# Four output quarters around the start of tile 1, the out-projection weights one place earlier, and a batch's score steps one block sooner, in a fused local-attention + SwiGLU kernel

## The chip, the cores and the metric

The kernel runs on one core of a Trainium2 chip. The metric is device time in microseconds (us), the median of five runs. Beside those five runs stands one profiled execution, whose trace gives every instruction's start and duration, and every DMA's issue and landing.

## What is computed

Two blocks follow each other. First comes attention with a sliding window of 96 keys and 8 global keys, with a bias that falls linearly with distance, over 4 batches, 8 heads, 768 positions and 64 features a head. Its output, read as 3072 tokens of 512 features, goes through a SwiGLU feed-forward block.

```python
keep = is_global | is_local                       # 8 first keys, or 0 <= rel < 96
scores = scale * q @ k.T - slopes * dist          # per head, masked where not keep
a = softmax(scores)
x = (a @ v).transpose(0, 2, 1, 3).reshape(3072, 512)
g = x @ w_gate                                    # 512 x 1536
out = (g * sigmoid(g) * (x @ w_val)) @ w_out      # 1536 x 512
```

## The kernel before, in words

**Tiles.** The 3072 tokens are cut in 8 tiles of 384 (t = 0 to 7), two tiles a batch. The 1536 hidden features are cut in 12 blocks of 128 (f = 0 to 11). I write (t, f) for block f of tile t. For each block `gate_or_val` runs four gate products and four value products (L547) into two PSUM banks. ScalarE then takes tanh of the gate (`th`, L558), VectorE makes `sl` from both (L560), and VectorE multiplies `sl` with the value product into `hT` (L564). Twelve `hT` blocks of a tile make three output groups of 128 tokens; each group is cut in four quarters of three matmuls (`out_part`, L576, into bank `o0`). A quarter reads three blocks of `hT` and one of four loads of `wo` (`load_wo(0)` to `load_wo(3)`, L218). After the fourth quarter ScalarE copies the bank out (`osb`, L582), and SyncE (SP) starts the write (L583). There are 96 quarters; `outs` lists those of tiles 0 to 6 in order, and the list `stretches` (L769 to L775) says after which block how many are taken. Before the change the first comes after (1,4), and one follows each block from (1,5) on, five of them at (1,11). The last three groups, those of tile 7, follow at the end.

**Attention steps between the blocks.** The attention of the next batch is cut into steps that TensorE runs between two blocks, at keys such as (t, 4), after that block's quarters, or (t, 11, 1), ahead of its quarter number 1. `tr` transposes q and k of two heads (L273; copies out on ScalarE L281, on VectorE L285 and L288). `sc` makes the scores of up to three units (L379); the exponentials (L387, ScalarE) of the first unit come at once, those of the others and all mask multiplications (L395, L398) are put on the list `later`. `va` makes denominators and numerators (L439), evicts the numerators (L470), and puts `invert` (L449, L450), `spread` (L455) and two scalings (L475, which write the next tile's `xT`) on `later`. `run_later` takes one entry off ahead of each gate, each value and each quarter; `take`, which starts a step, first empties the list. `first(1, 1)` places batch 1's steps in tile 1; batches 2 and 3 have theirs in `both`, at (t,0), (t,5), (t,8), (t+1,0), (t+1,4), (t+1,8) for t = 2 and 4.

**PSUM.** Gate and value products rotate over three banks (`spare`), over seven from (0,9) to (1,2) (`widen`, `narrow`). The first of three score units takes two of the same banks. So TensorE can start a value product only when the `sl` of the block before has been made, and scores only when the last gate's `sl` has.

**Loads.** GpSimd (POOL) issues the loads with a cast, in program order, on one queue: q and k of batch 0, v, weights, `wo` 0 and 1, then q and k heads 0 to 3 of batch 1, the global rows (L181), `wo` 2 and 3, q and k heads 4 to 7, v of batch 1. SP and ScalarE issue the first q and k heads, the identity, the distances and the first global v rows (L110 to L115). [...]

**Block 0's second half.** In tile 0 the steps `trh` and `sch` transpose and score the second half of batch 0; `trh(2, 3, True)` at (0,3) puts both qT copies (L330) on ScalarE, and `sch` puts the second half's exponentials (L361) on `later`.

Of the kernel before, what the change touches and what calls it, by code (L numbers as in the profile page):

```python
# [16 lines left out]
WIN = 216  # L17
# [20 lines left out]
def kernel(  # L38
# [12 lines left out]
    nc = tc.nc  # L51
# [18 lines left out]
    const_dr = nc.inline_tensor(  # L70
        np.concatenate([np.eye(128, dtype=np.float16), dist_np], axis=1), name="consts")
# [26 lines left out]
    dist = sb.tile([128, 3 * WIN], FP16, name="dist")  # L98
    J2 = TB // 128
    q32 = sb2.tile([128, 2, J2 * D], FP32, name="q32", tag="qst")  # L100
# [4 lines left out]
    def half_of(src, half, h0, h1):  # L105
        return src[0, h0:h1, TB * half:TB * half + TB, :].rearrange(
            "h (p j) d -> p h (j d)", p=128)
# [1 line left out]
    vG32 = sb.tile([NG, H, D], FP32, name="vG32")  # L109
    nc.sync.dma_start(out=k32, in_=half_of(k, 0, 0, 2))  # L110
    nc.scalar.dma_start(out=ident, in_=const_dr.ap()[:, 0:128])
    nc.scalar.dma_start(out=q32, in_=half_of(q, 0, 0, 2))
    nc.sync.dma_start(out=dist[:, 0:2 * WIN], in_=const_dr.ap()[:, 128:128 + 2 * WIN])
    nc.sync.dma_start(out=vG32, in_=v[0, :, 0:NG, :].rearrange("h p d -> p h d"))
    nc.sync.dma_start(out=dist[:, 2 * WIN:], in_=const_dr.ap()[:, 128 + 2 * WIN:])  # L115

# [30 lines left out]
    def stage(b):  # L147
        qst[b] = sb2.tile([128, H, J * D], FP16, name="qst", tag="qst")
        kst[b] = sb2.tile([128, H, J * D], FP16, name="kst", tag="kst")

    def load_qk(b, h0, h1):
        for st, src in ((kst[b], k), (qst[b], q)):
            nc.gpsimd.dma_start(
                out=st[:, h0:h1, :],
                in_=src[b, h0:h1].rearrange("h (p j) d -> p h (j d)", p=128))
# [23 lines left out]
    def load_globals():  # L179
        for dst, src in ((kG, k), (vG[:, 1:], v)):  # L180
            nc.gpsimd.dma_start(  # L181
                out=dst.rearrange("p b h d -> p (b h) d"),
                in_=src[1:, :, 0:NG, :].rearrange("b h p d -> p (b h) d"))

    def copy_globals(b):
        nc.sync.dma_start(
            out=vSs[b][0:NG],
            in_=vG[:, b, :, :].unsqueeze(1).broadcast_to([NG, NCH, H, D]))
# [28 lines left out]
    def load_wo(g):  # L217
        nc.gpsimd.dma_start(  # L218
            out=wo[:, 3 * g:3 * g + 3, :],
            in_=moe_w_out[384 * g:384 * g + 384].rearrange("(f p) d -> p f d", p=128))  # L220
# [18 lines left out]
    def banks(name, dt=FP32):  # L239
        return [bank(name, dt) for _ in range(2)]  # L240

    def spare(name, dt=FP32):
        tag = state["x"][gv.get("n", 0) % len(state["x"])]
        gv["n"] = gv.get("n", 0) + 1
        return single(name, tag, dt)

    def single(name, tag, dt=FP32):
        return ps.tile([128, 512 if dt == FP32 else 1024], dt, name=name, tag=tag)
# [6 lines left out]
    later = []  # L255

    def run_later(n):
        for _ in range(n):
            if later:
                later.pop(0)()  # L260
# [339 lines left out]
    pairs = {(b, hp): Pair(b, hp) for b in range(B) for hp in range(NP)}  # L600
    quads = {(b, g): Quad(b, g) for b in range(B) for g in range(2)}
    for c in range(3):
        load_v_rest(0, c)
    nc.gpsimd.dma_start(
        out=vCut[NG:NG + cut], in_=v[0, :, 3 * KC:TB, :].rearrange("h p d -> p h d"))
# [17 lines left out]
    def p_tr(hp, kt, qt, q_eng):  # L623
        tr = [single("trs", t, FP16)[:, 0:TB] for t in (qt, kt)]
        pairs[0, hp].turn_half(0, tr)
        pairs[0, hp].copy_half(0, tr, V, q_eng)

    V, A = nc.vector.tensor_copy, nc.scalar.copy
# [2 lines left out]
        make_slope(nc.scalar.mul, h)  # L631
    A(out=q16[:, 0, 0:2], in_=q32)
    V(out=k16[:, 0, 0:2], in_=k32)
    A(out=vG[:, 0], in_=vG32)
    copy_globals(0)
    nc.sync.dma_start(out=vCut[0:NG], in_=vG[:, 0])
    p_tr(0, "x0", "x1", A)
    for h in range(4, 8):
        make_slope(nc.vector.tensor_scalar_mul, h)
    load_w(0, 2)  # L640
# [6 lines left out]
    load_w(8, 12)  # L647
    load_wo(0)
    load_wo(1)
    stage(1)  # L650
    load_qk(1, 0, 4)
    load_globals()
    load_wo(2)
    load_wo(3)
    load_qk(1, 4, 8)
    for c in range(NCH):
# [29 lines left out]
    def sc(b, *units):  # L686
        def step():
            for i, (hp, bk, *other) in enumerate(units):
                pair = pairs[b + 1 if other else b, hp]
                on_vector = pair.b < 2 or bk < 2 or hp % 2 == 0  # L690
                exps, mask = pair.scores(
                    bk, nc.vector if on_vector else nc.gpsimd,
                    [spare("sc") for _ in range(2)] if len(units) == 3 and i == 0
                    else banks("sc"))
                if i == 0:
                    exps()
                else:
                    later.append(exps)
                later.append(mask)
        return step  # L700

    def va(b, g, half):
        return lambda: quads[b, g].values(half, bank, nc.vector)
# [4 lines left out]
    def tr(b, hp):  # L708
        return pairs[b, hp].transposes

    def trh(h0, h1, by_engine):
        def step():
            b0, b1 = single("trs", "o0", FP16), spare("trs", FP16)
            (a, b), (c, d) = [(t[:, 0:TB], t[:, TB:2 * TB]) for t in (b0, b1)]
            k_eng = V if by_engine else A
            pair_of = [(h0, (c, a)), (h1, (d, b))] if by_engine else [(h0, (b, a)), (h1, (d, c))]
            for hp, tr in pair_of:
                pairs[0, hp].turn_half(1, tr)
            for hp, tr in pair_of:
                pairs[0, hp].copy_half(1, tr, k_eng, A)  # L720
        return step

    def sch(hp):
        def step():
            p = pairs[0, hp]
            scs = [p.bias(1, 0), p.bias(1, 1)]
            for which in range(2):
                p.scores_half(1, which, scs[which], which == 1)
        return step

    def fetch(b, *hps):
# [7 lines left out]
    def first(t, b):  # L739
        return {(t, 2): [tr(b, 0), tr(b, 1)],  # L740
                (t, 4): [sc(b, (0, 0), (0, 1), (1, 0))],
                (t, 6): [tr(b, 2), tr(b, 3)],
                (t, 7): [sc(b, (1, 1), (2, 0), (2, 1))],
                (t, 9): [sc(b, (3, 0), (3, 1))],
                (t, 10): [va(b, 0, 0)],
                (t, 11, 1): [va(b, 1, 0)]}

    def both(t, b):

        n = b + 1  # L750
        return {(t, 0): [sc(b, (0, 2), (1, 2), (2, 2)), fetch(n, 0, 1)],
                (t, 5): [sc(b, (3, 2), (0, 0, n), (1, 0, n)), fetch(n, 2, 3)],
                (t, 8): [vas(b, 1)],
                (t + 1, 0): [sc(n, (0, 1), (1, 1), (2, 0))],
                (t + 1, 4): [sc(n, (2, 1), (3, 0), (3, 1))],
                (t + 1, 8): [vas(n, 0)]}

    def second(t, b):
        return {(t, 0): [sc(b, (0, 2), (1, 2))], (t, 3): [sc(b, (2, 2), (3, 2))],
                (t, 7): [vas(b, 1)]}  # L760

    half1 = {(0, 1): [trh(0, 1, False)], (0, 2): [sch(0)],
             (0, 3): [sch(1), trh(2, 3, True)], (0, 5): [sch(2)], (0, 6): [sch(3)],
             (0, 7): [va(0, 0, 1)], (0, 8): [va(0, 1, 1)]}

    def ff(t, f0, f1, n_out=(0,)):
        return [(t, f, n_out[(f - f0) % len(n_out)]) for f in range(f0, f1)]

    stretches = [  # L769
        (ff(0, 0, 12), half1),  # L770
        (ff(1, 0, 5, (0, 0, 0, 0, 1)) + ff(1, 5, 11, (1,)) + [(1, 11, 5)], first(1, 1)),
        (ff(2, 0, 12, (1,)) + ff(3, 0, 12, (1,)), both(2, 1)),
        (ff(4, 0, 12, (1,)) + ff(5, 0, 12, (1,)), both(4, 2)),
        (ff(6, 0, 12, (1,)), second(6, 3)),
        (ff(7, 0, 12, (1,)), {})]  # L775

    loads, after = {}, {}

# [105 lines left out]
```

The softmax here doesn't subtract the row's maximum and nothing guards it: scores larger than these inputs give would overflow.

## Time and profile before

| what | value |
|---|---|
| median of five runs (lowest to highest) | 244.96 us (243.76 to 245.14) |
| the profiled execution: its own time, and the span of its trace | 244.84 us, 243.1 us |
| granted TensorE clock | 1.00 |
| PE (TensorE) busy | 234.5 us, 96% of the span |
| VectorE (DVE), ScalarE (ACT), GpSimd busy | 165.9, 129.6, 96.7 us |
| gate and value products, L547 | 77.1 and 76.6 us |
| output quarters, L576 | 72.8 us |

The 1.7 us between the span and the execution's own time lie outside the first and last instruction. Busy times of PE overlap, since matmuls are pipelined; what a matmul costs is the distance from its start to the next one's: four products of 384 columns take 0.65 us, a quarter (three matmuls of 512 columns) 0.64 us. In a timeline row the first number is the start, the second the duration of the group of like instructions, and in brackets stands the engine's idle time ahead of it with what ended it.

### The profile page before, as it was taken

How to read it: one execution, taken by the hardware profiler on the slowest of the kernel's cores; microseconds unless marked ns; L12 is line 12 of the kernel's file. 1: busy time of each engine (PE TensorE's matmuls, PEld its weight loads, DVE VectorE, ACT ScalarE, POOL GpSimd, SP SyncE). 2: the span in 40 equal slices, each digit the busy share in tenths (PEclk: the TensorE clock that was granted, in tenths of full speed). 3: DMA queues.
4: the chain of work that ended last, by engine and by line, in shares of the span. 5: the costliest groups of instructions: out<-in, count | busy, mean ns of one | idle time of the engine just before them, and what ended most of it. 6: DMA issues, size and time to landing. Idle time of an engine off the chain costs nothing.

```text
span 243.1 us, 6052 instructions
## 1 busy us (share of the span) xinstructions
PE 234.5 (96%) x2428; PEld 135.5 (56%) x2428; DVE 165.9 (68%) x354; ACT 129.6 (53%) x295; POOL 96.7 (40%) x117
## 2 busy tenths in 40 slices
PE   8799899799999999999999999999999999999994
PEld 4456566455555556555565556555655565555543
DVE  5675749879796768776786658776785568555610
ACT  5548586786864565366346464367336634333221
POOL 8998674728980000996062252700032213000000
PEclk9999999999999999999999999999999999999999
DMA  7999999999999585799309877941101101110122
GB/s 145 167 181 198 180 206 198 203 156 127 147 122 148 122 133 97 49 158 143 57 5 148 143 140 87 71 65 44 46 0 46 43 6 39 45 43 1 44 89 86
DMA packets 84612, 25.10 MB, mean 103 GB/s; under 512 B 72816, under 2 KB 81640, under 8 KB 84584
## 3 DMA queue, kind: packets, MB, share of 16 engines
q0 software_dynamic: 65296, 14.05, 66.6%
q1 hardware_dynamic: 18728, 10.30, 17.3%
q8 instruction: 19, 0.31, 0.5%
q10 hardware_dynamic: 560, 0.36, 0.5%
q14 instruction: 9, 0.07, 0.1%
HBM read 28.67 MB, written 6.29 MB: 144 GB/s over the span
## 4 chain that ended last, share of the span: by engine, by line
PE 84%; DMA 6%; POOL 5%; DVE 2%; issue 1%; ACT 0%; DVEq 0%; POOLq 0%
PE gps L547 25%; PE vps L547 24%; PE ops L576 23%; DMA wv<-in_moe_w_val_dram 3%; PE sc L379 3%; PE num L439 3%; DMA vS<-in_v_dram 3%; PE den L439 2%; POOL q L119 1%; PE trs L273 1%; POOL wg L213 1%; PE ops L592 1%; POOL k L119 1%; POOL wv L213 1%; DVE xT L475 1%
## 5 line engine op out<-in xcount | busy, mean ns | idle before, releaser
L547 PE MATMUL gps<-xT,wg 128*128 128x384 f16 x376 | 77.1, 327 | 2.1 <-DVE hT L564 1.7
L560 DVE SCALAR_TENSOR_TENSOR sl<-th,gps 128x384 f32<-128x384 f32 x94 | 52.0, 553 | 39.5 <-ACT th L558 39.2
L547 PE MATMUL vps<-xT,wv 128*128 128x384 f16 x376 | 76.6, 326 | 0.5 <-DMA wv<-in_moe_w_val_dram 0.4
L558 ACT ACTIVATE th<-gps 128x384 f32<-128x384 f32 x94 | 46.9, 499 | 52.7 <-PE gps L547 51.4
L576 PE MATMUL ops<-wo,hT 128*128 128x512 f16 x276 | 72.8, 379 | 0.0
L564 DVE TENSOR_TENSOR hT<-vps,sl 128x384 f16<-128x384 f32 x94 | 52.1, 554 | 8.7 <-DVE sl L560 0.5
L547 PEld LDWEIGHTS <-wg 128*128 128x128 f16 x384 | 35.1, 98 | 33.1 <-issue 3.6
L547 PEld LDWEIGHTS <-wv 128*128 128x128 f16 x384 | 37.5, 98 | 26.6 <-issue 1.3
L576 PEld LDWEIGHTS <-hT 128*128 128x128 f16 x276 | 26.9, 98 | 23.8
L387 ACT ACTIVATE at<-sc 128x432 f16<-128x432 f32 x72 | 33.2, 538 | 11.5 <-PE sc L379 11.5
L516 POOL TENSOR_TENSOR xT<-ns,rb 128x384 f16<-128x384 f32 x10 | 9.8, 995 | 66.5 <-DVE rb L455 55.5
L171 POOL DMA_DIRECT2D vS<-in_v_dram x28 | 24.7, 893 | 5.8 <-DMA kst<-in_k_dram 4.1
L582 ACT ACTIVATE osb<-ops 128x512 f32<-128x512 f32 x23 | 13.7, 597 | 22.0 <-PE ops L576 22.0
L398 POOL TENSOR_TENSOR at<-at,masks 128x864 f16<-128x864 f16 x4 | 7.3, 1822 | 23.8 <-ACT at L387 19.1
L398 DVE TENSOR_TENSOR at<-at,masks 128x864 f16<-128x864 f16 x20 | 12.1, 605 | 5.7 <-ACT at L387 5.7
L194 POOL DMA_DIRECT2D kst<-in_k_dram x16 | 13.9, 885 | 2.3 <-PE vps L547 1.7
L361 ACT ACTIVATE at<-sc 128x432 f16<-128x432 f32 (+2 forms) x32 | 11.7, 446 | 5.3 <-PE sc L350 5.3
L194 POOL DMA_DIRECT2D qst<-in_q_dram x16 | 13.7, 878 | 0.0
L512 ACT COPY ns<-num 128x384 f32<-128x384 f32 x20 | 8.1, 492 | 7.9 <-PE num L439 7.9
L439 PE MATMUL num<-at,vS 128*32 128x216 f16 (+6 forms) x560 | 11.1, 226 | 0.0
L395 DVE TENSOR_TENSOR at<-at,masks 128x432 f16<-128x432 f16 x24 | 8.1, 378 | 4.3 <-ACT at L387 4.3
L449 DVE STREAM_TRANSPOSE dT<-den 128x384 f32<-128x384 f32 x16 | 9.3, 581 | 1.6 <-PE den L439 1.1
(74 smaller groups left out, 178.5 us busy)
## 6 DMA issues: line engine op xcount, KB each, us to landing
out_dram<-osb SPq DMA_DIRECT2D x23, 256.0 KB
vS<-in_v_dram POOLq DMA_DIRECT2D x24, 120.0 KB, 5.8
wo<-in_moe_w_out_dram POOLq DMA_DIRECT2D x4, 384.0 KB, 10.4
qst<-in_q_dram POOLq DMA_DIRECT2D x16, 96.0 KB, 4.2
kst<-in_k_dram POOLq DMA_DIRECT2D x16, 90.0 KB, 4.2
wg<-in_moe_w_gate_dram POOLq DMA_DIRECT2D x4, 256.0 KB, 7.7
wv<-in_moe_w_val_dram POOLq DMA_DIRECT2D x4, 256.0 KB, 7.8
kst<-in_k_dram POOLq DMA_DIRECT2D x2, 384.0 KB, 12.1
```

The costliest lines, as they stand in the source:

```text
L171: nc.gpsimd.dma_start(out=vSs[b][NG:NG + n, c, :, :], in_=v[b, :, KC * c:KC * c + n, :].rearrange("h p d -> p h d"))
L194: nc.gpsimd.dma_start(out=st[b][p0:p0 + n, h // 2, :, h % 2, :], in_=src[b, h, 0:n * J].rearrange("(t p) d -> p t d", p=n))
L361: nc.scalar.activation(out=at[:, hi, 0:col + n], in_=sc[hi][:, 0:col + n], func=AF.Exp, scale=scale)
L387: nc.scalar.activation(out=at[:, hi, :], in_=sc[hi][:, 0:BANK], func=AF.Exp, scale=scale)
L398: mul_eng.tensor_mul(at, at, m[:, :, o:o + BANK])
L439: nc.tensor.matmul(dst[r, o:o + n], lhsT=ones[:, 0:32] if side is None else vals[:, 4 * g + j, side::2], rhs=pairs[b, 2 * g + j // 2].at[c ...
L547: nc.tensor.matmul(gv[f, which][:, 0:TB], lhsT=w[:, c, 128 * f:128 * f + 128], rhs=x_of(t)[:, c, :], start=(c == 0), stop=(c == NC - 1))
L558: nc.scalar.activation(out=th, in_=dst[:, 0:TB], func=AF.Tanh, scale=0.5)
L560: nc.vector.scalar_tensor_tensor(out=sl, in0=th, scalar=1.0, in1=dst[:, 0:TB], op0=AluOp.add, op1=AluOp.mult)
L564: nc.vector.tensor_mul(hTs[t][:, f, :], dst[:, 0:TB], gv["sl"])
L576: nc.tensor.matmul(ops, lhsT=hTs[t][:, f, 128 * i:128 * i + 128], rhs=wo[:, f, :], start=(f == 0), stop=(f == NFF - 1))
L582: nc.scalar.mul(out=osb, in_=ops, mul=0.5)
```

## The change

1. **Head.** On SP's queue the distances change places with the first q heads, which ScalarE's queue issued: q now follows k on SP, and the distances follow the identity on ScalarE. The cast of the global v rows moves behind the first qT copy in ScalarE's order; SP's copies of those rows (L186, L636) follow it.
2. **Tile 0.** In the step at (0,3) the second qT copy moves from ScalarE to VectorE, and the exponentials of heads 2 and 3 are no longer put off.
3. **Quarters.** One quarter comes after each of (0,10), (0,11), (1,0), (1,2). Then one comes after each of (1,4) to (1,9), and two after (1,10) and (1,11). Tile 1 takes two more by its end than before, so that from tile 2 on every quarter in the list stands two places earlier and (7,10) and (7,11) have none.
4. **Loads.** `load_wo(2)` comes ahead of batch 1's q and k.
5. **Batch 1's steps.** All but the first two come one block sooner, and the last one empties `later` at once.

```diff
-    nc.scalar.dma_start(out=q32, in_=half_of(q, 0, 0, 2))
-    nc.sync.dma_start(out=dist[:, 0:2 * WIN], in_=const_dr.ap()[:, 128:128 + 2 * WIN])
+    nc.scalar.dma_start(out=dist[:, 0:2 * WIN], in_=const_dr.ap()[:, 128:128 + 2 * WIN])
+    nc.sync.dma_start(out=q32, in_=half_of(q, 0, 0, 2))
...
+    p_tr(0, "x0", "x1", A)
     A(out=vG[:, 0], in_=vG32)
     copy_globals(0)
     nc.sync.dma_start(out=vCut[0:NG], in_=vG[:, 0])
-    p_tr(0, "x0", "x1", A)
...
     load_wo(1)
+    load_wo(2)
     stage(1)
     load_qk(1, 0, 4)
     load_globals()
-    load_wo(2)
     load_wo(3)
...
-            k_eng = V if by_engine else A
+            k_eng, last = (V, V) if by_engine else (A, A)
...
-                pairs[0, hp].copy_half(1, tr, k_eng, A)
+                pairs[0, hp].copy_half(1, tr, k_eng, A if hp == h0 else last)
...
-                p.scores_half(1, which, scs[which], which == 1)
+                p.scores_half(1, which, scs[which], which == 1 and hp != 1)
...
                 (t, 4): [sc(b, (0, 0), (0, 1), (1, 0))],
-                (t, 6): [tr(b, 2), tr(b, 3)],
-                (t, 7): [sc(b, (1, 1), (2, 0), (2, 1))],
-                (t, 9): [sc(b, (3, 0), (3, 1))],
-                (t, 10): [va(b, 0, 0)],
-                (t, 11, 1): [va(b, 1, 0)]}
+                (t, 5): [tr(b, 2), tr(b, 3)],
+                (t, 6): [sc(b, (1, 1), (2, 0), (2, 1))],
+                (t, 8): [sc(b, (3, 0), (3, 1))],
+                (t, 9): [va(b, 0, 0)],
+                (t, 10, 1): [va(b, 1, 0), lambda: run_later(len(later))]}
...
-        (ff(0, 0, 12), half1),
-        (ff(1, 0, 5, (0, 0, 0, 0, 1)) + ff(1, 5, 11, (1,)) + [(1, 11, 5)], first(1, 1)),
+        (ff(0, 0, 10) + ff(0, 10, 12, (1,)), half1),
+        (ff(1, 0, 4, (1, 0)) + ff(1, 4, 10, (1,)) + ff(1, 10, 12, (2,)), first(1, 1)),
...
-        (ff(7, 0, 12, (1,)), {})]
+        (ff(7, 0, 10, (1,)) + ff(7, 10, 12), {})]
```

More of the change, by code (lines that the diff above doesn't have):

```diff
@@ L692, in step @@
                     bk, nc.vector if on_vector else nc.gpsimd,
-                    [spare("sc") for _ in range(2)] if len(units) == 3 and i == 0
+                    [spare("sc") for _ in range(2)] if i == 0 and len(units) == 3
                     else banks("sc"))
```

## The prediction

> **What bounds the kernel now.** I read the page's slices first, then busy time by stage, then what TensorE (PE) waits for, then the timelines around each PE wait.
>
> ```profile
> PE   8799899799999999999999999999999999999994
> PEclk9999999999999999999999999999999999999999
> ```
> ```profile
> 28.00:44.00 16.00, 16.00 (x225) 9.97 (x224) 12.06 (x25) 10.88 (x28) 9.08 (x13) 1.00 1.36 199
> 44.00:47.00 3.00, 1.25 (x8) 0.66 (x7) 2.69 (x6) 1.62 (x5) 3.00 (x4) 1.00 1.25 204
> ```
> ```profile
> PE gps L547 <- DVE hT L564: 1.7, 1, 1.7
> ```
> ```profile
> 43.49 0.81 PE L547 MATMUL vps<-xT,wv 128*128 128x384 f16 x4
> 46.05 0.81 PE L547 MATMUL gps<-xT,wg 128*128 128x384 f16 x4 [1.75 <-DVE hT L564]
> ...
> 50.22 0.81 PE L547 MATMUL gps<-xT,wg 128*128 128x384 f16 x4
> 51.05 0.81 PE L547 MATMUL vps<-xT,wv 128*128 128x384 f16 x4
> ```
>
> PE is full in nearly every slice at full clock (the stage rows give length, then busy time and count of PE, PEld, DVE, ACT, POOL, then clock, DMA share, GB/s). In 44 to 47 us PE works 1.25 of 3.00 us while VectorE works 2.69: VectorE, still behind from scaling x for tile 1, frees no PSUM bank. So only PE's idle time is to be won. I take it start to start: a product begins 0.16 us after the one before, so the value product of 43.49 gives PE free at 44.14, and the gate of 46.05 comes 1.91 us late. At 51.05 the value starts 0.18 late (0.83 after its gate, not 0.65). At tile 2's first gate, (2,0), the fourth matmul waits for the last xT piece, 74.47 to 75.03: 0.30 late. From there to the end I find no start-to-start gap but about 0.10 wherever PE changes between full and smaller matmul shapes, and the change leaves their number alone. **At most 1.91 + 0.18 + 0.30 = 2.39 us can be won.**
>
> Ahead of 28 us PE waits for weights: its gate of 25.61 stops for wg (0.41 late) and the value product stops for wv until 27.62 (0.61). That chain is one load after another on POOL's queue.
>
> **The change, part by part.**
>
> *Head: 0.* PE's slack ahead of the weights is 0.41 + 0.61 = 1.0 us. ScalarE's cast of q waited 0.68 us, to 4.67, for q; its issue moves from 1.16 on ScalarE's queue to about 1.26 on SP's, behind k. [...] The vG cast (0.61) moves from 5.09 to about 6.1, ahead of the exponentials of 6.92; the copies SP issued at 5.73 and 6.64 come 1 us later and are read at 13.44. At (0,3) a qT copy goes from ScalarE (0.48) to VectorE (0.55), and exponentials (0.97) move ahead of a tanh: PE is waiting for weights there. 0.
>
> *Quarters in the gap.* A quarter is 3 x 213 ns = 0.64 us. With VectorE's order unchanged, PE runs: gate and value of (0,10) to 40.24, quarter to 40.88, (0,11) to 42.18, quarter to 42.82, (1,0) to 44.12, quarter to 44.76, (1,1) to 46.06. The gate of (1,2) then asks for its bank at 46.06 and VectorE frees it at 46.00 as before: the gap of 1.91 is filled by three quarters (1.92). `wo` loads 0 and 1 were issued at 28.80 and 29.79 with landings 8.8 and 9.7 us later (37.6, 39.5): in time. Load 2 takes the place of k's, 1.9 us behind load 1 (the spacing of two 384 KB loads): 41.4, in time for 44.12.
>
> The fourth quarter, after (1,2), is ready at 47.36 and needs load 3:
>
> ```profile
> 36.00 0.78 POOL L218 DMA_DIRECT2D wo<-in_moe_w_out_dram  x1 [0.42 <-DMA wv<-in_moe_w_val_dram]
> ```
> ```profile
> DMA to landing us min/median/max: 8.8/10.4/11.7
> ```
>
> 36.00 + 11.7 = 47.7. The bytes ahead of it on the queue are the same, so PE waits to 47.77: **-0.41** (between 0 and 1.0, should the order change its landing by half a us). Behind it wait the transposes, which start at 48.51 instead of 47.44. k and q of heads 0 to 3 land 1.9 later than their 41.5 and 43.6: in time. The bank wait of 51.05 shrinks to 0.04. So four quarters (2.56) are done for a lag of 0.93 at the scores of (1,4) (53.37 instead of 52.44): 1.91 + 0.18 - 0.41 - 0.04 = **+1.64**.
>
> *Output write.* The first 256 KB write now leaves SP near 49.2, and the globals' copies, issued at 44.46 before, are queued behind it; they are read after 65. q of heads 4 to 7 was issued at 39.82 and landed 14.3 later, 54.1; it is now read at 56.4. [...]
>
> *Transposes one block sooner.* They stood after (1,6), when all exponentials and masks of (1,4) were through. After (1,5) two entries are still on the list, and `take` runs them first: one pair of exponentials ahead of the kT copies, one mask (0.52) ahead of qT.
>
> ```profile
> 57.54 0.55 DVE L564 TENSOR_TENSOR hT<-vps,sl 128x384 f16<-128x384 f32 x1
> 58.01 0.95 DVE L285 COPY qT<-trs 128x768 f16<-128x768 f16 x1
> 58.88 0.17 DVE L288 COPY kT<-kT 128x56 f16<-128x56 f16 x1
> 58.96 0.95 DVE L285 COPY qT<-trs 128x768 f16<-128x768 f16 x1
> 59.82 0.32 DVE L288 COPY kT<-kT 128x56 f16<-128x56 f16 x1
> 59.94 0.56 DVE L560 SCALAR_TENSOR_TENSOR sl<-th,gps 128x384 f32<-128x384 f32 x1
> ```
>
> Before, transposes began at 57.09, this `sl` ended at 60.50, and the scores that take its bank started at 60.61: no slack left. After, transposes begin at 53.37 + 2.71 = 56.08. ScalarE's two exponential pairs run 55.28 to 57.07, masks 56.55 to 57.67 on VectorE, qT from 57.67: 1.59 behind the transposes, not 0.92. `sl` then ends at 57.67 + 2.49 = 60.16, the scores are due at 59.60: **-0.57** (0 to 1.1; about half if the mask overlaps, double if ScalarE slips by a kT pair).
>
> *Last steps sooner.* The values now follow (1,9) and (1,10), and the list is emptied at once. Before, from the start of the first values (67.80), the last xT ended at +7.23 and (2,0)'s fourth gate matmul was due at about +6.97. After, VectorE's order to xT is nearly the same (two pieces of hT work exchanged), and (2,0) starts at +7.10, its fourth matmul at +7.58: **+0.30**. `sl` and `hT` of (1,11) are queued behind the xT work; the `sl` ends at +7.70, and (2,0)'s value wants that bank at +7.75. No slack, but no wait.
>
> *Two places ahead for the rest.* Fourth quarters fall on f = 1, 5, 9 instead of 3, 7, 11. At (2,0), (3,0), (3,4) and the same places of tiles 4 and 5 the ScalarE copy `osb` (0.60, some 0.49 of the queue) now lies between the exponentials just put out and the next tanh:
>
> ```profile
> 78.17 0.49 ACT L558 ACTIVATE th<-gps 128x384 f32<-128x384 f32 x1 [0.17 <-PE gps L547]
> 78.55 1.79 ACT L387 ACTIVATE at<-sc 128x432 f16<-128x432 f32 x4
> 80.19 0.53 ACT L558 ACTIVATE th<-gps 128x384 f32<-128x384 f32 x1
> ```
>
> That queue is full; the tanh of 80.19 slips by 0.49 and by 0.09 for the quarter's end. Its `sl` ended at 81.32 and the value that needs the bank began at 81.86: slack 0.49 beside 0.05 of signalling. Six times 0.58 - 0.49: **-0.5** (0 to 1.2). (7,10) and (7,11) without quarters: 0.05 at one bank. The tail's own quarters cover the last hT (0.65 + 3 x 0.64 against 1.95).
>
> Sum: 1.64 - 0.57 + 0.30 - 0.5 - 0.05 = **0.82 us won**. Against the profiled execution, 244.84 - 0.82 = 244.02; the median stands 0.12 above that execution, so 244.96 - 0.82 = **244.1 us**.
>
> **Rivals.**
>
> *All won.* The tile 1 stall and the `osb` stalls do not appear, as `sl` runs a little sooner than I queue it: 0.82 + 0.57 + 0.5 = 1.89, 243.1 us. For it: both are differences of a few tenths. Against it: no slack in the `sl` of 59.94.
>
> [...]
>
> *Slower: full queues.* Work put ahead of a tanh or an `sl` in an order that cannot be changed costs more than the overlap I allow: 1.1 at the tile 1 scores and 0.25 at each of six places is 2.6 instead of 1.07, so 0.7 lost: 245.7 us. It decides once these places cost over 1.9 together. For it: the queues are full just there. Against it: the row of 0.49 slack.
>
> **How the numbers follow.** A measurement of this kernel tells about 0.3% (0.73 us) from no change. Forecast 0.44 (243.6 to 244.7, about half of it past 244.2 towards faster); all won 0.20; moved 0.16; slower 0.20. Faster 0.44 x 0.5 + 0.20 = 0.42; slower 0.18; same 0.40. The range, 243.0 to 245.6, reaches into both outer cases.
>
> **What would show it.** The PE wait for hT near 46 is gone; a wait for wo of about 0.4 near 47.4; scores of block (1,6) late by 0.6; no wait at (2,0); value products one block after (2,0), (3,0), (3,4) late by under 0.1. I am wrong if the fourth quarter waits over 1 us, if transposes wait for q, or if the `osb` places cost over 0.2 each.

## The result, and the profile after

The changed kernel takes 244.0 us (median of 28 runs, 243.19 to 246.35) against 244.84 us (47 runs of the kernel before): ratio 0.9973, interval 0.9962 to 0.9985. By the ratio 0.66 us are won (0.37 to 0.93); the two medians lie 0.84 apart; 0.82 was forecast. The profiled execution took 243.99 us, its span 242.2.

PE's slices, and the stage row that answers to the gap's (length; busy time and count of PE, PEld, DVE, ACT, POOL; clock, DMA share, GB/s). The slices, 6.1 us each, read as before: they are too coarse for a gap of 1.9 us; the row shows it closed.

```profile
PE   8899799999999999999999999999999999999994
```
```profile
44.00:47.00 3.00, 3.00 (x19) 1.72 (x18) 2.63 (x6) 2.11 (x6) 1.35 (x2) 1.00 1.36 194
```

VectorE still works 2.63 of these 3.00 us: it was not relieved, PE was given something else to do. The timeline of PE around the old gap (start, duration of the group):

```profile
44.61 0.81 PE L576 MATMUL ops<-wo,hT 128*128 128x512 f16 x3
45.25 0.81 PE L547 MATMUL gps<-xT,wg 128*128 128x384 f16 x4
45.90 0.81 PE L547 MATMUL vps<-xT,wv 128*128 128x384 f16 x4
46.55 0.81 PE L547 MATMUL gps<-xT,wg 128*128 128x384 f16 x4
47.24 0.81 PE L547 MATMUL vps<-xT,wv 128*128 128x384 f16 x4
47.88 0.81 PE L576 MATMUL ops<-wo,hT 128*128 128x512 f16 x3
```

The starts are 0.64, 0.65, 0.65, 0.69, 0.64 apart: no gap above 0.04. The fourth quarter starts as soon as its value product is through; the wait for `wo` that I forecast is not there. What the waits of PE show instead is the head (first the lines of before, then those of the changed kernel: us in all, times, longest):

```profile
PE gps L547 <- DMA wg<-in_moe_w_gate_dram: 0.2, 1, 0.2
PE vps L547 <- DMA wv<-in_moe_w_val_dram: 0.4, 1, 0.4
```
```profile
PE gps L547 <- DMA wg<-in_moe_w_gate_dram: 0.7, 1, 0.7
PE vps L547 <- DMA wv<-in_moe_w_val_dram: 0.7, 1, 0.7
```

The value product that ends PE's wait for weights starts at 28.09, not at 27.62 as before. So I compare two numbers per trace: when that product starts (**weights**), and the span from there on (**rest**), which hardly depends on how early the weights came (214.09 and 214.07 with weights at 28.09 and 29.02). e1 to e4, e5 to e8, e9 to e11 and e12 ran on four chips, each beside its own runs of the kernel before (medians 244.84, 244.85, 244.71 and 245.24 us); from row to row compare the ratios, not the times. One of e11's six runs (246.16 us, clock 0.992) counts as slow and is not in its ratio.

| kernel | time, us | ratio (interval) | weights | rest |
|---|---|---|---|---|
| before | 244.84 | 1 | 27.62 | 215.44 |
| changed | 244.0 | 0.9973 (0.9962-0.9985) | 28.09 | 214.09 |
| e1, head as before | 243.83 | 0.9961 (0.9945-0.9976) | 29.02 | 214.07 |
| e2, before with the new head | 244.91 | 1.0009 (0.9994-1.0025) | 27.57 | 215.56 |
| e3, output copy put off | 250.5 | 1.0231 (1.0205-1.0258) | 27.75 | 221.09 |
| e4, e3 with wo sooner, old head | 250.28 | 1.0218 (1.0190-1.0246) | 27.06 | 220.98 |
| e5, gap filled, nothing else | 245.94 | 1.0038 (1.0020-1.0056) | 27.88 | 215.47 |
| e6, steps as before | 246.47 | 1.0057 (1.0033-1.0081) | 27.60 | 218.10 |
| e7, two orders at the transposes | 243.37 | 0.9937 (0.9915-0.9960) | 27.83 | 213.74 |
| e8, quarters back in phase | 243.99 | 0.9960 (0.9945-0.9976) | 27.38 | 214.20 |
| e9, steps sooner alone | 245.1 | 1.0024 (1.0005-1.0043) | 27.51 | 215.69 |
| e10, third wo load late | 245.15 | 1.0024 (1.0004-1.0044) | 27.56 | 215.76 |
| e11, e7 with wo sooner | 243.2 | 0.9930 (0.9904-0.9957) | 27.83 | 213.60 |
| e12, e11 with the old head | 242.82 | 0.9899 (0.9871-0.9927) | 27.62 | 213.60 |

In the profiled executions the rest fell by 215.44 - 214.09 = 1.35, and weights that came 0.47 later took part of it back.

### The profile page after: what moved, and what is told of

It reads as the page before. It is cut to its first block, busy times and chain, and to the rows that moved or that the text cites. A ratio compares the mean times of both kernels' runs of the same rounds, so it can differ in the third digit from the quotient of the medians.

```text
span 242.2 us, 6053 instructions
## 1 busy us (share of the span) xinstructions
PE 235.2 (97%) x2428; PEld 135.7 (56%) x2428; DVE 165.9 (69%) x355; ACT 129.2 (53%) x294; POOL 96.7 (40%) x117
## 4 chain that ended last, share of the span: by engine, by line
PE 87%; DMA 8%; POOL 2%; ACT 1%; issue 1%; POOLq 0%
PE gps L547 26%; PE vps L547 25%; PE ops L576 24%; DMA wv<-in_moe_w_val_dram 6%; PE sc L379 3%; PE num L439 3%; DMA vS<-in_v_dram 3%; PE den L439 2%; PE trs L273 1%; PE ops L592 1%; POOL vS L171 1%; POOL k L119 1%; POOL q L119 1%; PE sc L339 0%; ACT at L387 0%
## 5 line engine op out<-in xcount | busy, mean ns | idle before, releaser
L560 DVE SCALAR_TENSOR_TENSOR sl<-th,gps 128x384 f32<-128x384 f32 x94 | 51.9, 552 | 39.9 <-ACT th L558 39.1
L387 ACT ACTIVATE at<-sc 128x432 f16<-128x432 f32 x72 | 33.9, 533 | 10.8 <-PE sc L379 10.8
```

The costliest lines, as they stand in the source:

```text
L387: nc.scalar.activation(out=at[:, hi, :], in_=sc[hi][:, 0:BANK], func=AF.Exp, scale=scale)
L560: nc.vector.scalar_tensor_tensor(out=sl, in0=th, scalar=1.0, in1=dst[:, 0:TB], op0=AluOp.add, op1=AluOp.mult)
```

## The experiments

**e1 and e2: the head.** e1 puts the head back in the changed kernel; e2 is the kernel before with the new head alone.

```diff
-    nc.scalar.dma_start(out=dist[:, 0:2 * WIN], in_=const_dr.ap()[:, 128:128 + 2 * WIN])
-    nc.sync.dma_start(out=q32, in_=half_of(q, 0, 0, 2))
+    nc.scalar.dma_start(out=q32, in_=half_of(q, 0, 0, 2))
+    nc.sync.dma_start(out=dist[:, 0:2 * WIN], in_=const_dr.ap()[:, 128:128 + 2 * WIN])
...
+    A(out=vG[:, 0], in_=vG32)
+    copy_globals(0)
+    nc.sync.dma_start(out=vCut[0:NG], in_=vG[:, 0])
     p_tr(0, "x0", "x1", A)
-    A(out=vG[:, 0], in_=vG32)
-    copy_globals(0)
-    nc.sync.dma_start(out=vCut[0:NG], in_=vG[:, 0])
```

> The changed kernel with the head as before: first q heads on ScalarE's queue, distances on SP's, the vG cast ahead of the first qT copy. In the changed kernel's trace the last weights that TensorE waits for ahead of 28 us landed at 28.04 instead of 27.57, and the fourth quarter found its wo load already there. Theory: the head edit made the weights 0.47 later, and the wait for the fourth wo load, which I had put at 0.41, was hidden under it. Then with the head back the weights land near 27.6, the fourth quarter waits about 0.4 for wo, and the time stays within 0.15 of the changed kernel: 243.9 to 244.1. Rival 1: the head costs and nothing hides it: 0.4 to 0.5 faster, 243.5. Rival 2: the later weights are chance of one execution: weights land anywhere from 27.5 to 28.1, time 244.0, and the wait for wo is there only when they land early.

> The kernel before with only the head edited (queues exchanged, vG cast behind the first qT copy). Theory: the head edit itself delays the weights; wv lands near 28.0, everything behind it moves along, 0.3 to 0.5 slower than before: 245.2. Rival (chance): wv lands near 27.6 and the time is that of before within 0.15: 244.8.

My theory that the head edit made the weights late falls. With the old head the wait for the weights ended even later, at 29.02; with the new head on the old kernel at 27.57. PE's waits of e1:

```profile
PE gps L547 <- DMA wg<-in_moe_w_gate_dram: 1.4, 1, 1.4
PE vps L547 <- DMA wv<-in_moe_w_val_dram: 0.7, 1, 0.7
```

Over all traces the wait ends at 27.06 to 29.02 with the old head (before, e1, e4, e5, e12; mean 27.84) and at 27.38 to 28.09 with the new (nine traces; mean 27.68). The landing scatters by more than the edit moves it: the second rival was right, though the scatter is wider than its 27.5 to 28.1. The rests of pairs that differ in the head agree (214.09 and 214.07; 215.44 and 215.56).

**e3 and e4: the output copy behind the tanh.** The six late value products are there in the changed kernel as forecast; e3 tries to be rid of them. e4 adds the old head and both late `wo` loads ahead of q and k.

```diff
-            nc.scalar.mul(out=osb, in_=ops, mul=0.5)
-            nc.sync.dma_start(out=out[r0:r0 + 128, :], in_=osb)
+            def evict():
+                nc.scalar.mul(out=osb, in_=ops, mul=0.5)
+                nc.sync.dma_start(out=out[r0:r0 + 128, :], in_=osb)
+            if t == NT - 1:
+                evict()
+            else:
+                later.insert(min(2, len(later)), evict)
```

> The changed kernel with the ScalarE copy of a finished output group put on the list of put-off work, at most two entries deep, so that it comes behind the exponentials and the next tanh. Theory: the six value products that begin 0.07 late at two blocks after (2,0), (3,0), (3,4), (4,0), (5,0), (5,4) are on time again, 0.4 us won: 243.6. Rival: the copy only moves and another bank comes late for it (the one output bank must be free three instructions groups later): 244.0 or slower.

> The changed kernel with the head as before, the fourth wo load also ahead of batch 1's q and k, and the output copy put off as in the run with that alone. Theory: the three terms add: weights 0.47 sooner, no wait for wo (both late wo loads land by 43.5), 0.4 from the six places: 243.1. q of heads 0 to 3 of batch 1 lands near 47.4 and is read at 48.4, so no new wait. Rival: q and k, two loads later, hold up the first transposes by more than is won: 244.0 or more.

The rival held, by far: 1.0231. PE and ScalarE in e3:

```profile
80.40 0.81 PE L547 MATMUL vps<-xT,wv 128*128 128x384 f16 x4
81.76 0.81 PE L576 MATMUL ops<-wo,hT 128*128 128x512 f16 x3 [0.55 <-ACT osb L584]
```
```profile
80.68 0.53 ACT L558 ACTIVATE th<-gps 128x384 f32<-128x384 f32 x1
81.05 0.65 ACT L584 ACTIVATE osb<-ops 128x512 f32<-128x512 f32 x1
```

ScalarE takes the two in the program's order: tanh at 80.68, copy at 81.05. The next quarter follows the one just done by a gate and a value, 1.3 us; behind the tanh the copy of the only output bank ends 0.7 too late. Eleven quarters wait so, 0.58 or 0.71 each. The 0.07 gaps are gone, and 7 us are lost. In e4 the weights came early and the fourth `wo` wait was absent, but the copy decides that run too.

**e5: the gap filled, and nothing else.** The third `wo` load moves as in the change (not shown below); three quarters move from (1,11) into the gap.

```diff
-        (ff(0, 0, 12), half1),
-        (ff(1, 0, 5, (0, 0, 0, 0, 1)) + ff(1, 5, 11, (1,)) + [(1, 11, 5)], first(1, 1)),
+        (ff(0, 0, 10) + ff(0, 10, 12, (1,)), half1),
+        (ff(1, 0, 4, (1, 0, 0, 0)) + ff(1, 4, 11, (1,)) + [(1, 11, 2)], first(1, 1)),
```

> The kernel before with the wo load moved as in the change and three quarters taken after (0,10), (0,11) and (1,0), at the cost of three of the five at (1,11); attention steps, head and every later quarter as before. Theory: the gap near 46 is filled (1.9 won), but the quarters at (1,11) had covered the chain of batch 1's last values to xT on VectorE, some 4.3 from those values to xT against 2.0 of work now left ahead of the fourth matmul of (2,0): (2,0) waits 2.3 instead of 0.3, and the time is that of before within 0.2: 244.8. So in the change it is the steps one block sooner, and two quarters drawn from the end, that keep the gain. Rival: idle time once filled is won: 1.9 faster, 242.9.

```profile
72.65 0.54 PE L547 MATMUL gps<-xT,wg 128*128 128x384 f16 x2
74.90 0.79 PE L547 MATMUL gps<-xT,wg 128*128 128x384 f16 x2 [1.71 <-DVE xT L475]
```

The gap went to (2,0): the third matmul starts 1.87 late and the fourth 0.31 more, 2.2 in all where 2.3 was forecast. The rest, 215.47, is that of before, as the theory says. The measured time is not: by the ratio 0.93 us above before, in runs from 244.40 to 247.43. The last section takes that up.

**e6 and e9: the steps.** e6 takes the changed kernel with `first` as before. e9 keeps the sooner steps and takes the early quarters away:

```diff
-        (ff(0, 0, 10) + ff(0, 10, 12, (1,)), half1),
-        (ff(1, 0, 4, (1, 0)) + ff(1, 4, 10, (1,)) + ff(1, 10, 12, (2,)), first(1, 1)),
+        (ff(0, 0, 12), half1),
+        (ff(1, 0, 4) + ff(1, 4, 10, (1,)) + [(1, 10, 2), (1, 11, 4)], first(1, 1)),
...
-        (ff(7, 0, 10, (1,)) + ff(7, 10, 12), {})]
+        (ff(7, 0, 12, (1,)), {})]
```

> The changed kernel with batch 1's steps at the blocks where they were before (transposes after (1,6), scores after (1,7) and (1,9), values after (1,10) and (1,11) ahead of its second quarter). Theory: TensorE's late starts around the second transposes and their scores, 0.55 together, go, but (2,0) waits 2.2 for xT: 1.6 slower than the changed kernel, 245.6. Rival: the sooner steps only save the 0.3 of (2,0) and cost 0.55: without them 0.2 faster, 243.7.

> The changed kernel without its early quarters: none ahead of (1,4), one after each of (1,4) to (1,9), two after (1,10), four after (1,11), one after every later block; steps sooner, loads and head as changed. Theory: the gap of 1.9 near 46 is back, the late starts at the second transposes (0.35 to 0.55) stay, the 0.3 at (2,0) is gone, and the six 0.07 gaps are gone since each quarter stands where it stood before: within 0.3 of the kernel before, 244.6 to 245.1. Rival: the sooner steps bring the gain: 244.0.

e6 lost more than forecast: 246.47. Its rest is 4.0 above that of the changed kernel. From PE's start-to-start distances: 2.2 at (2,0) as forecast, a wait for the fourth `wo` load of 0.7 before the first transposes, 0.5 less at the second ones; the remaining 1.6 goes with a clock that halved (last section). e9 came as forecast: its waits of PE begin with

```profile
PE gps L547 <- DVE hT L564: 1.7, 1, 1.7
```

So the steps alone bring nothing (1.0024), the gap filled alone brings nothing, and the two together do. Part 2 of the change, in tile 0, is never taken alone; its copies and exponentials run ahead of the last weights (24.5 to 27.5 us), and e9's rest comes out without it: 215.44, less 0.30 at (2,0), and 0.55 more at the second transposes, make its 215.69.

**e7 and e11: the late starts at the second transposes.** k's transposes take the PSUM bank whose scores are read out first by the exponentials (in every `tr` step), and the mask comes after the hT of (1,6); e11 also moves the fourth `wo` load ahead of batch 1's q and k.

```diff
-            trq, trk = (t[:, 0:S] for t in banks("trs", FP16))
+            trk, trq = (t[:, 0:S] for t in banks("trs", FP16))
...
+        keep = getattr(step_list[0], "keep", 0)
+        held = [later.pop() for _ in range(keep)][::-1]
         run_later(len(later))
         for step in step_list:
             step()
+        later.extend([lambda: None] * (2 * keep) + held)
```

The step after (1,5) runs both transposes with keep = 1 (not shown).

> The changed kernel with two edits at the transposes after (1,5): k's transposes take the first of each two PSUM banks instead of q's (the first is read out of its exponentials earlier), and the mask multiplication that stood ahead of the qT copies on VectorE comes after the hT of (1,6). Theory: the late starts of transposes (0.20 and 0.05) and scores (0.18 with the wait for the last gate's bank) come from these two queue places and go: 0.4 to 0.55 won against the changed kernel, 243.5. Rival: ScalarE's exponentials set the time, not the bank order or the mask: 244.0.

> The changed kernel with the bank order and mask order of the run that had these alone, and the fourth wo load also ahead of batch 1's q and k. Theory: the fourth quarter's wait for wo, 0.0 to 0.2 in the traces so far, is gone and nothing else changes: equal to the run with the two orders alone or 0.15 faster, 243.3. Rival: q of heads 0 to 3, one load later, holds up the first transposes: 243.8 or slower.

VectorE in the changed kernel, and in e7:

```profile
57.23 0.60 DVE L398 TENSOR_TENSOR at<-at,masks 128x864 f16<-128x864 f16 x1
57.75 0.95 DVE L285 COPY qT<-trs 128x768 f16<-128x768 f16 x1
...
59.65 0.55 DVE L560 SCALAR_TENSOR_TENSOR sl<-th,gps 128x384 f32<-128x384 f32 x1
```
```profile
57.12 0.95 DVE L285 COPY qT<-trs 128x768 f16<-128x768 f16 x1
...
59.01 0.55 DVE L560 SCALAR_TENSOR_TENSOR sl<-th,gps 128x384 f32<-128x384 f32 x1
59.66 0.56 DVE L564 TENSOR_TENSOR hT<-vps,sl 128x384 f16<-128x384 f32 x1
60.14 0.60 DVE L398 TENSOR_TENSOR at<-at,masks 128x864 f16<-128x864 f16 x1
```

With the mask out of the way `sl` starts at 59.01, and in e7 the transposes start 0.33 to 0.36 apart without a hole. The rest falls by 0.35 although e7 shows a `wo` wait of 0.15 that the changed kernel's trace lacks: 0.5 together, as the theory had it. No run splits the two edits. e11 drops that wait too (rest 213.60); its time cannot be told from e7's.

**e8: the phase.**

```diff
-        (ff(2, 0, 12, (1,)) + ff(3, 0, 12, (1,)), both(2, 1)),
+        (ff(2, 0, 3, (1,)) + ff(2, 3, 5) + ff(2, 5, 12, (1,)) + ff(3, 0, 12, (1,)), both(2, 1)),
...
-        (ff(7, 0, 10, (1,)) + ff(7, 10, 12), {})]
+        (ff(7, 0, 12, (1,)), {})]
```

> The changed kernel without quarters after (2,3) and (2,4), two more at the end, so that from (2,5) on each quarter stands where it stood before. Theory: five of the six late value products (0.07 each), all but that after (2,0), are gone; 0.05 may come back at (2,4): 0.3 faster than the changed kernel, 243.7. Rival: those gaps are not from the place of the output copy: 244.0, gaps as they are.

```profile
82.29 0.81 PE L547 MATMUL gps<-xT,wg 128*128 128x384 f16 x4 [0.18 <-DVE hT L564]
```

Five of the six 0.07 gaps are gone, so they do come from the copy's place. But a gate next to the two bare blocks now starts 0.34 late (at 82.29, waiting for `hT`): without quarters PE runs into VectorE's queue there. I had allowed 0.05. Its trace also has 0.10 of the `wo` wait. Rest 214.20: nothing won.

**e10: the third wo load.** The changed kernel with `load_wo(2)` where it was.

> The changed kernel with the third wo load behind batch 1's global rows, where it was. Theory: the third early quarter, due near 44.7, waits for a landing near 45.9; the steps behind it come 1.2 later, the fourth quarter and the first transposes with them: 0.9 to 1.3 slower than the changed kernel, 245.1. Rival: VectorE frees no bank until 46 anyway, and the wait lies in that gap: within 0.2 of it, 244.0.

```profile
45.74 0.81 PE L576 MATMUL ops<-wo,hT 128*128 128x512 f16 x3 [1.50 <-DMA wo<-in_moe_w_out_dram]
```

The third quarter is 1.67 late, and the rest 1.67 above the changed kernel's: no part of the wait lies in VectorE's gap. Forecast 0.9 to 1.3 above the changed kernel, measured 1.15 between the medians and 1.25 between the ratios. Without this one line the change would lose.

**e12: the head once more.**

> The version with the two orders at the second transposes and the fourth wo load sooner, now with the head as before the change. Theory: the head edit is worth nothing, since the weights' landing ahead of 28 us scatters by more than it could move: within 0.3 of that version, a ratio to the kernel before of 0.992 to 0.994. Rival: the head edit delays the loads by some 0.3 us, as the two earlier comparisons would allow: 242.9, a ratio under 0.992.

0.9899 against 0.9930 for e11: the rival's number and not the theory's, though the intervals overlap. Both traces have a rest of 213.60. The three pairs by time (e1 and changed, e2 and before, e12 and e11) all have the new head slower, by 0.12, 0.09 and 0.31%, none clear of its interval; the traces show no later weights with it. Whether the head edit costs some 0.2 to 0.3 us, as e1 and e2 would have it, stays open. e12 is the fastest version run: 242.82 us.

## Why the prediction was right, step by step

- *Gap filled by three quarters, 1.91:* shown. The gap is gone in the changed kernel and back in e9.
- *The bank wait at (1,4), 0.18 to 0.04:* the value starts 0.68 after its gate, 0.03 late.
- *Wait of the fourth quarter for wo, 0.41:* 0.0 in this execution. I had held both the landing, 47.7, and PE's start fixed. Here weights and PE moved 0.47 while `wo` landed at 36.10 + 11.7 = 47.8. In e1 the wait is 0 too, in e3, e7 and e8 0.10 to 0.15, in e6 0.7. The term is the difference of two landings on one queue; my 0.41 lies inside its range, and no single number stands for it.
- *Second transposes one block sooner, 0.57:* the sum was right (0.5 by e7 and e11), the place half wrong. I put all of it on `sl`; in the trace

```profile
56.38 0.53 PE L273 MATMUL trs<-ident,kst 128*64 128x128 f16 x12
56.71 0.53 PE L273 MATMUL trs<-ident,qst 128*64 128x128 f16 x12
57.22 0.53 PE L273 MATMUL trs<-ident,kst 128*64 128x128 f16 x12
```

  the transposes themselves start 0.20 late and are held 0.15 at 57.22. ScalarE runs four exponentials from 55.38 to 57.17, and the banks that the transposes take hold the scores that these read; I had counted them only as being ahead of the kT copies. The scores then lose the remaining 0.2.
- *Values sooner, 0.30 at (2,0):* shown; the gate of 74.57 runs without a wait, that of before (first line) lasts 0.3 longer. e5 and e6 show what it is worth with the quarters gone from (1,11): 2.2.

```profile
74.30 1.10 PE L547 MATMUL gps<-xT,wg 128*128 128x384 f16 x4
```
```profile
74.57 0.81 PE L547 MATMUL gps<-xT,wg 128*128 128x384 f16 x4
```

- *Output copies ahead of the tanh, six times 0.09, put down as 0.5 in all:* six times 0.07, 0.42 in all. ScalarE and PE in the changed kernel:

```profile
78.54 0.95 ACT L387 ACTIVATE at<-sc 128x432 f16<-128x432 f32 x2
79.45 0.60 ACT L582 ACTIVATE osb<-ops 128x512 f32<-128x512 f32 x1
79.94 0.95 ACT L387 ACTIVATE at<-sc 128x432 f16<-128x432 f32 x2
80.76 0.51 ACT L558 ACTIVATE th<-gps 128x384 f32<-128x384 f32 x1
```
```profile
81.19 0.81 PE L547 MATMUL gps<-xT,wg 128*128 128x384 f16 x4
81.91 0.81 PE L547 MATMUL vps<-xT,wv 128*128 128x384 f16 x4
```

  The tanh came at 80.76 (80.19 before), 0.57 later against 0.58 forecast; the value starts 0.72 after its gate, not 0.65.
- *Head, 0:* no effect in the traces, but the weights' landing scattered over 1.96 us (27.06 to 29.02), far above the 0.68 that ScalarE's cast had waited for q. I had taken one execution's landing as given.
- *Output write and q's landing:* no run has PE waiting for q there; in the changed kernel q landed at 39.98 + 11.9 = 51.9 and was read at 56.71. The chance of 0.16 for "moved" counts on a cost here beside a long wait for `wo`: no run shows a cost at q's landing, and the longest wait for the fourth load was 0.7 (e6).

The rest came out at 214.09 where my terms make 215.44 - 0.82 = 214.62. Of the difference, 0.41 is the `wo` wait, 0.08 the copies, and 0.05 the bank at (7,10) or (7,11), where the trace has no wait. So the path was right, and the costs but for the `wo` wait; the profile shows 1.35 won behind the weights.

That the measured gain, 0.66 to 0.84, lies so near 0.82 is in part luck. In the pair of profiled executions, weights that came 0.47 later hide part of the 1.35. In ordinary runs the weights need not come late (mean 27.68 with the new head), and yet these gained no more. A `wo` wait as in e3, e6, e7 and e8, and a cost of the head as in e1, would each take some tenths; neither is shown for ordinary runs, and what takes the remainder isn't settled.

## What to carry to other kernels

Idle time of the bounding engine is won only if the work put there isn't cover for another chain: list what the moved work hid where it stood, and move the chain with it (e5 alone 1.0038, e9 alone 1.0024, both in the change 0.9973). On ScalarE, which in e3 kept to the program's order (tanh at 80.68, copy at 81.05), and with one output bank, a copy has two neighbours that can stall, the one it delays and the one that waits for it; compare both slacks (0.49 and below zero here) before moving it. Compare executions by what comes behind their last wait for loads, since that wait alone ends anywhere within 2 us here (27.06 to 29.02).

## What was not expected of the hardware

The clock halved after a wait. In e6, around its 2.2 us at (2,0):

```profile
73.50:77.00 3.50, 1.65 (x19) 0.65 (x12) 3.25 (x7) 0.83 (x2) 0.62 (x1) 1.00 1.97 126
77.00:80.40 3.40, 3.40 (x16) 1.40 (x17) 1.11 (x2) 0.49 (x1) 0.00 (x0) 0.50 0.05 3
80.40:84.00 3.60, 3.60 (x35) 2.19 (x30) 2.24 (x4) 3.29 (x8) 0.00 (x0) 1.00 0.52 101
```

PE was granted half its clock for 3.4 us, and the row counts 16 matmuls where the next stretch, hardly longer, has 35.

The same wait did not always bring that. e5 has 2.2 us at (2,0) too, and keeps its clock:

```profile
73.30:76.70 3.40, 1.65 (x9) 0.77 (x8) 2.29 (x6) 0.64 (x2) 0.00 (x0) 1.00 0.29 82
76.70:80.10 3.40, 3.40 (x35) 2.03 (x34) 2.29 (x5) 2.59 (x7) 0.00 (x0) 1.00 0.32 62
```

So does the kernel before over its gap of 1.91: 1.00 from 44 to 47 us, with PE at work for 1.25 of the 3.00, and 1.00 from 47 to 76. PE is busy for 1.65 of 3.50 us in the row ahead of e6's half clock and for 1.65 of 3.40 in e5's first row, which full clock follows: what decides is not shown.

Half clock goes with most of e5's surplus. Every run lists its mean clock, and 3.4 us at half clock in some 245 us would make 0.993, which is what e6's trace has. Of e5's 22 runs, 12 stand at 0.993, with a median of 246.36 us, and ten at 1.00, with 245.29; of the 57 runs of before beside them, one stands at 0.993, and the others have 244.81. So about 0.6 of the 0.93 goes with the clock, and the gap filled alone still wins nothing at full clock. In e6 7 of 15 runs stand at 0.991 to 0.993 (246.98); the other eight have 245.75, where 245.6 was forecast. Where in a run the half clock lay, these lists don't tell. A gap of 2 us in PE can thus cost more than itself: in e6's trace 2.2 us and 1.6 more.
